# Output tiles of an attention and gated-MLP kernel: separate loads for the last query chunk, late tiles in spare weight buffers, another rule table

## The chip, the core and the metric

The kernel runs on one core of a Trainium2 chip. The metric is the device time of one execution in microseconds (us), lower is better. A profile of one execution shows each engine: PE (TensorE, matmuls), ACT (ScalarE), DVE (VectorE), POOL (GpSimd), SP (SyncE, which issues most DMA transfers).

## What is computed

```python
# x: (1, 2048, 640) bf16;  32 heads of 20;  F = 1728
xn  = layernorm(x)
q, k, v = split_heads(xn @ wqkv)
s   = (softmax(q @ k.T * 20**-0.5) @ v).merge_heads() @ wo
h   = sigmoid(xn @ w_gate) * (xn @ w_up)
g   = silu(h @ w_down)
out = x + s * g
```

The exponentials are the bulk: 32 heads x 2048 queries x 2048 keys. With tiles of 128 keys by 512 queries that is 32 x 4 x 16 = 2048 tiles.

## The kernel before

The kernel works in **blocks**: a block is a group of four heads (`g`, 0 to 7) with a chunk of 512 queries (`c`, 0 to 3), 32 blocks in all. Blocks 0 to 23 go group by group. From block 24 (`PAIR`) on, groups 6 and 7 alternate, so block 25 finishes chunk 0, block 27 chunk 1, block 29 chunk 2 and block 31 chunk 3.

The order of the instructions on PE, ScalarE and VectorE is made when the program is built, by a list scheduler that keeps a clock `now` of its own and rough durations. It chooses for PE among score matmuls ("F"), products with V ("PV") and **filler** items ("M": projections, the MLP, the output projection), and gives each score tile to ScalarE (an exponential, 2 tiles at a time, with a third in a spare PSUM bank when there is one) or to VectorE (`iv`, then three bit-level passes over four tiles). A table `PLAN` holds one row of rules for each block:

```python
RULE = dict(urgent=0.25, rounds=4, hold=0.15, slack=0.2, s0=0.2, s1=0.2, wait3=0.4, fall=1, lag=0.0,
            dmax=2, third=2, dord=0, mord=0, mfew=2, npv=4, held=48, burst=1, excl=1, dl=20, dle=8)
```

For instance, `s0` and `s1` say how far VectorE's queue may reach ahead when it is given a tile, `wait3` how long a fill may wait for a third bank, `mfew` how many PSUM banks filler may take, `lag` how far the filler may be behind.

The output: attention results go to DRAM (`oD`) when a block is normalised, and come back as `o_mid` (chunks 0 to 2) or `o_end` (chunk 3, the first 480 of 640 rows; the rest is done in the tail). The gate values `g` go to DRAM (`gq_dram`) and come back with x in an *out tile*.

```python
    def load_out(tt):                        # out tile of 128 queries: x and the gate
        if tt in out_tiles:
            return
        o2 = xfl[:, tt % 2 * KD * QC:tt % 2 * KD * QC + 3 * D]      # two buffers, in xnT
        ...                                  # two loads on nc.sync
        ev_at[("ol", tt)] = now + 4.0

    def mk_out(tt, h, at):                   # one half of an output tile, chunks 0 to 2
        def alloc():
            if h == 0:
                load_out(tt)
            st["ps"] = misc_ps()
        def mm(kd): ...                      # 5 matmuls 128x320
        def ev():
            ...                              # VectorE: otmp = 0.25 * psum * gate
            ...                              # GpSimd: x + otmp
            if h == 1:
                nc.sync.dma_start(out=out2[...], in_=xr)
                if tt + 2 < TT - 4 and ...:
                    load_out(tt + 2)

    def mk_part(t4, h, at):                  # chunk 3: the first 480 rows of its projection, 4 matmuls
        ...
            nc.vector.scalar_tensor_tensor(out=tmp, in0=st["ps"][:, 0:HD], scalar=0.25, in1=gqr, ...)
            nc.gpsimd.tensor_tensor(out=xps[t4][:, sl], in0=tmp, in1=tail[t4][:, sl], op=ALU.add)
        ...
            pre=[all of chunk 3's down-projection, ("wo",), ("oc", NQC - 1), ("xr",)]
    ...
        if b == NBLK - 2:                    # the parts enter the list of items
```

`xps` lies in the buffer of the down-projection weights, `wd`, once these are no longer needed.

Normalisation of a block (`norm_a`, `norm_b`, `norm_c`): VectorE copies the sums `on` out of PSUM, the denominators go through DRAM, VectorE takes the reciprocal `rt`, this goes through DRAM again and comes back as `rl`; a 1x1 memset on `rl` by VectorE releases GpSimd's multiply `on_bf`, which is stored to `oD`. The times of the steps are set by the scheduler:

```python
    timed.append((free["DVE"] + 7.0, ...) + norm_a(...))            # reciprocal 7 us after the copy
    gos.append((now + GO_AT, tm[1], tm[2], rl))                     # GO_AT = 9.0
    if ... gos[0][0] <= now and (two tiles wait for DVE or now > gos[0][0] + GO_WAIT):   # GO_WAIT = 8.0
```

The tail, after the last exponential: ScalarE copies the last block's sums, PE transposes, VectorE divides, PE transposes back, ScalarE copies (`o7`). Then "early" matmuls (block 30's heads) and "late" ones (block 31's) fill four banks; VectorE and GpSimd combine these with gates, parts and x, and the last tiles are stored. The early matmuls wait until no filler item is left in their bank.

Of the kernel before, what the change touches and what calls it, by code (L numbers as in the profile page):

```python
# [18 lines left out]
P = 128  # L19
HEADS = 32  # L20
GH = 4
NG = HEADS // GH
DH = 20
GC = GH * DH
QC = 512
# [20 lines left out]
    (0.25, 5, 0.15, 0.2, 0.5, 0.2, 0.4, 1, 0.0, 2, 2, 0, 0, 3, 4, 48, 0, 1, 20, 8),  # L46
    (0.25, 5, 0.15, 0.2, 0.5, 0.2, 0.2, 1, 0.0, 2, 2, 0, 0, 3, 4, 48, 0, 0, 20, 8),
    (0.25, 5, 0.15, 0.2, 0.5, 0.2, 0.4, 1, 0.0, 2, 2, 0, 0, 3, 4, 48, 0, 1, 28, 8),
    (0.25, 5, 0.15, 0.2, 0.5, 0.2, 0.4, 1, 14.0, 2, 2, 0, 0, 3, 4, 48, 0, 1, 20, 8),
    (0.25, 5, 0.15, 0.2, 0.5, 0.5, 0.4, 1, 14.0, 2, 2, 0, 0, 3, 4, 48, 0, 1, 20, 8),  # L50
    (0.25, 7, 0.15, 0.2, 0.2, 1.2, 0.4, 1, 0.0, 2, 2, 1, 0, 2, 4, 48, 1, 1, 20, 8),
    (0.25, 5, 0, 0, 0.5, 0.2, 0.4, 1, 14.0, 2, 2, 0, 0, 3, 4, 64, 0, 1, 20, 8),
    (0.25, 5, 0.15, 0.2, 0.5, 0.5, 0.4, 1, 14.0, 2, 2, 0, 0, 3, 4, 48, 0, 1, 28, 8),
    (0.2, 5, 0.15, 0.2, 0.5, 0.5, 0.4, 1, 14.0, 1, 0, 0, 2, 3, 4, 48, 0, 1, 28, 8),
    (0.25, 5, 0.15, 0, 0.5, 0.5, 0.4, 1, 14.0, 2, 2, 0, 0, 3, 4, 48, 0, 1, 28, 8),
    (0.25, 5, 0.15, 0, 0.5, 0.5, 0.4, 1, 14.0, 2, 2, 0, 0, 3, 4, 48, 0, 1, 28, 8),
    (0.25, 5, 0.15, 0, 0.5, 1.2, 0.4, 1, 14.0, 2, 2, 0, 0, 3, 4, 48, 0, 1, 20, 8),
    (0.25, 5, 0.15, 0, 0.5, 1.2, 0.4, 1, 2.0, 2, 2, 0, 1, 3, 4, 48, 0, 1, 20, 8),
    (0.3, 5, 0.15, 0, 0.5, 0.5, 0.4, 1, 14.0, 2, 2, 0, 0, 3, 4, 48, 0, 1, 28, 8),
    (0.25, 5, 0.15, 0, 0.5, 1.2, 0.4, 1, 2.0, 2, 2, 0, 1, 3, 4, 48, 0, 1, 28, 8),  # L60
    (0.3, 5, 0.15, 0.2, 0.5, 0.5, 0.4, 1, 14.0, 2, 2, 0, 0, 3, 4, 48, 0, 1, 28, 8),
    (0.25, 5, 0.15, 0, 0.5, 1.2, 0.4, 1, 4.0, 2, 2, 0, 1, 3, 4, 40, 0, 0, 28, 8),
    (0.25, 5, 0.15, 0, 0.5, 1.2, 0.4, 1, 4.0, 1, 2, 0, 1, 3, 4, 40, 0, 0, 14, 8),
    (0.25, 7, 0.15, 0, 0.5, 1.2, 0.4, 1, 4.0, 1, 2, 0, 1, 3, 4, 40, 0, 0, 14, 8),
    (0.25, 5, 0.15, 0, 0.5, 1.2, 0.4, 1, 4.0, 2, 2, 0, 1, 1, 4, 40, 0, 0, 28, 8),
    (0.2, 5, 0.15, 0, 0.8, 1.2, 0.4, 1, 4.0, 2, 2, 0, 1, 1, 4, 40, 0, 0, 28, 8),
    (0.25, 5, 0.15, 0.5, 0.5, 1.2, 0.4, 1, 4.0, 2, 2, 0, 1, 1, 4, 40, 0, 0, 28, 8),
    (0.25, 5, 0, 0, 0.5, 1.2, 0.4, 1, 4.0, 2, 2, 0, 2, 1, 4, 40, 0, 0, 28, 8),
    (0.25, 5, 0.15, 0, 0.5, 1.2, 0.4, 1, 4.0, 2, 2, 1, 3, 1, 4, 40, 0, 0, 28, 8),
    (0.25, 5, 0.15, 0, 0.5, 1.2, 0.4, 1, 0.0, 2, 0, 1, 3, 1, 4, 40, 0, 0, 28, 8),  # L70
    (0.25, 5, 0.15, 0, 0.2, 1.2, 0.4, 1, 0.0, 2, 0, 1, 3, 1, 4, 40, 1, 0, 28, 8),
    (0.25, 5, 0.15, 0, 0.2, 1.2, 0.4, 1, 0.0, 2, 0, 1, 3, 1, 4, 56, 1, 0, 28, 8),
    (0.25, 5, 0.15, 0, 0, 1.2, 0.4, 1, 0.0, 2, 2, 1, 3, 1, 4, 4, 1, 0, 28, 8),
# [38 lines left out]
def kernel(  # L112
# [11 lines left out]
    nc = tc.nc  # L124
# [360 lines left out]

    def blk(g, c):
        return g * NQC + c if g < NG - 2 else PAIR + 2 * c + g - (NG - 2)
# [297 lines left out]
    def load_out(tt):  # L785
        if tt in out_tiles:
            return
        o2 = xfl[:, tt % 2 * KD * QC:tt % 2 * KD * QC + 3 * D]
        out_tiles[tt] = (o2[:, 0:D], o2[:, D:3 * D].bitcast(FP32))
        nc.sync.dma_start(out=out_tiles[tt][0], in_=x2[tt * P:(tt + 1) * P, :])  # L790
        nc.sync.dma_start(out=out_tiles[tt][1], in_=gq_dram[tt * P:(tt + 1) * P, :])
        ev_at[("ol", tt)] = now + 4.0
# [5 lines left out]
    def mk_out(tt, h, at):  # L798
        st = {}

        def alloc():
            if h == 0:
                load_out(tt)
            st["ps"] = misc_ps()
# [6 lines left out]
        def ev():  # L811
            xr, gqr = out_tiles[tt]
            sl = slice(h * HD, (h + 1) * HD)
            tmp = w2.tile([P, HD], FP32, tag="gqs", bufs=3, name="otmp")
            nc.vector.scalar_tensor_tensor(out=tmp, in0=st["ps"][:, 0:HD], scalar=0.25,  # L815
                                           in1=gqr[:, sl], op0=ALU.mult, op1=ALU.mult)
            add = nc.vector if h == 1 and claimed[0] == NJOB * NBLK else nc.gpsimd
            add.tensor_tensor(out=xr[:, sl], in0=tmp, in1=xr[:, sl], op=ALU.add)  # L818
            if h == 1:
                nc.sync.dma_start(out=out2[tt * P:(tt + 1) * P, :], in_=xr)  # L820
                if tt + 2 < TT - 4 and all(("d", (tt + 2) // 4, t4, i) in ev_at for t4 in range(4) for i in range(2)):
                    load_out(tt + 2)
        return Item([("PE", alloc, [(0.136, lambda kd=kd: mm(kd)) for kd in range(KD)]),
                     ("DVE", 0.40, ev, "free", lambda t: (mark("o", tt, h)(t), pool_hold(t)))], at, need=blk(NG - 1, tt // 4),
                    pre=[("d", tt // 4, t4, i) for t4 in range(4) for i in range(2)] + [("wo",), ("oc", tt // 4)] + (
                        [("o", tt - 2, 1)] if h == 0 and tt > 1 else []), gates={1: [("ol", tt)]})
# [37 lines left out]
    for b in range(NBLK):  # L864
# [20 lines left out]
        if b == NBLK - 2:  # L885
            for t4 in range(4):
                for h in range(2):
                    mk.append(lambda at, t4=t4, h=h: [mk_part(t4, h, at)])
# [231 lines left out]
    with tc.manual_schedule(engines={ENG.PE, ENG.Activation, ENG.DVE}):  # L1120
# [22 lines left out]
        o_next = 0  # L1143
# [41 lines left out]
        while chain or items or glu_items or o_next < NQC or any(it.i < len(it.ops) for it in active):  # L1185
# [10 lines left out]
            if ("wo",) not in ev_at and base() >= PAIR and ("bD", NU - 1) in ev_at and all(  # L1196
# [3 lines left out]
                load_out(0)  # L1200
                load_out(1)
# [5 lines left out]
            if o_next < NQC and o_at.get(blk(NG - 1 if o_next < NQC - 1 else NG - 3, o_next), 1e9) <= now and (  # L1207
                    all(ev_at.get(("o", 4 * o_next - 4 + i, 1), 1e9) <= now for i in range(4)) if 0 < o_next < NQC - 1 else
                    o_next == 0 or all(ev_at.get(("h", 3, kf), 1e9) <= now for kf in range(NFT))):
                o_rows = D if o_next < NQC - 1 else FE  # L1210
                for kd in range(-(-o_rows // P)):
                    r = min(P, o_rows - kd * P)
                    nc.sync.dma_start(out=(o_mid if o_next < NQC - 1 else o_end)[0:r, kd, :],
                                      in_=oD[kd * P:kd * P + r, o_next * QC:(o_next + 1) * QC])
                ev_at[("oc", o_next)] = now + 4.0
                o_next += 1
            if not tail and base() >= NBLK - 4:
                tail_load()
                ev_at[("xr",)] = now + 5.0
            active = [it for it in active if it.i < len(it.ops)]  # L1220
# [19 lines left out]
            for eng in ("ACT", "DVE"):  # L1240
# [8 lines left out]
                if eng == "DVE" and norm_pending is not None and norm_pending[1] <= now and norm_pending[0] < NBLK - 1:  # L1249
                    free["DVE"] = now + T_ON  # L1250
                    timed.append((free["DVE"] + 7.0, norm_pending[0]) + norm_a(norm_pending[0]))
# [4 lines left out]
                if eng == "DVE" and gos and gos[0][0] <= now and (  # L1256
                        sum(x[3] <= now + 0.3 for x in dq) >= 2 or now > gos[0][0] + GO_WAIT):
# [39 lines left out]
                if tm is not None:  # L1297
# [7 lines left out]
                    else:  # L1305
                        gos.append((now + GO_AT, tm[1], tm[2], rl))
# [217 lines left out]
```

## Time and profile before

| | before |
|---|---|
| time, median of 3 | 808.75 us (806.73 to 809.88) |
| profiled span | 804.8 us |
| PE / VectorE / ScalarE / GpSimd busy | 761.6 / 777.5 / 777.7 / 90.5 us |
| mean granted TensorE clock | 0.987 |
| DMA | 62.62 MB, mean 78 GB/s |

In the page, a group's row reads: line, engine, operation, output <- input, shape, count, then busy time in total, mean ns of one, and the engine's idle time before it with what ended it. A window's row gives, for each engine, busy us and the number of instructions, then the granted clock as a share of full speed, the busy share of the DMA engines and GB/s. A timeline's row gives start, duration, engine, line, operation and count; in brackets stands the idle time before it and what ended it.

### The profile page before, as it was taken

To read this page: it belongs to the slowest core of one execution; us is meant where nothing else is said; L and a number is where in the kernel's file an instruction comes from. 1 tells how busy PE (TensorE), PEld (TensorE's weight loads), DVE (VectorE), ACT (ScalarE), POOL (GpSimd) and SP (SyncE) were. 2 spreads that over 40 slices of the span, in tenths; PEclk is the share of its full clock that TensorE was granted. 3 is DMA by queue.
4 is the path that set the end of the run, shared out by engine and by line. 5 is a ranking of instruction groups with operands and counts; after the bars stand their busy time and mean duration, and the time that the engine had idled before them with its cause. 6 is when DMAs were issued, how large, how long until landed. Compare 5 with 4: busy or idle time off the path is not lost.

```text
span 804.8 us, 17176 instructions
## 1 busy us (share of the span) xinstructions
PE 761.6 (95%) x6458; PEld 274.8 (34%) x6514; DVE 777.5 (97%) x1280; ACT 777.7 (97%) x1005; POOL 90.5 (11%) x106
## 2 busy tenths in 40 slices
PE   7899999999999999999999999999999999989795
PEld 6522323233332333344322333343333333322233
DVE  8899999999999999999999999999999999999996
ACT  8899999999999999999999999999999999999892
POOL 6000000000000000000000000000000000411426
PEclk9999999999999999999999999999999999998898
DMA  6511231223122333212223333232143220340522
GB/s 167 172 49 48 68 79 43 70 66 83 56 77 65 79 88 100 69 36 59 62 54 99 84 81 88 60 103 85 46 115 94 48 55 17 89 116 23 176 72 72
DMA packets 95876, 62.62 MB, mean 78 GB/s; under 512 B 36388, under 2 KB 89684, under 8 KB 95792
## 3 DMA queue, kind: packets, MB, share of 16 engines
q1 hardware_dynamic: 95504, 61.18, 27.8%
q8 instruction: 51, 0.84, 0.5%
q14 instruction: 33, 0.27, 0.1%
q10 hardware_dynamic: 288, 0.33, 0.1%
HBM read 47.84 MB, written 13.55 MB: 76 GB/s over the span
## 4 chain that ended last, share of the span: by engine, by line
ACT 66%; PE 22%; issue 5%; DVE 5%; DMA 2%; POOL 0%; SPq 0%; DVEq 0%; ACTq 0%; POOLq 0%
ACT pt L142 59%; PE scA L934 7%; PE bk L970 5%; PE bk L749 5%; ACT tnh L142 3%; PE bk L711 2%; DVE iv L1313 1%; ACT td L142 1%; PE bk L808 1%; DVE pb L1028 1%; ACT sq L338 1%; ACT xnT L362 1%; ACT sq L336 1%; DVE pb L1025 0%; PE bk L934 0%
## 5 line engine op out<-in xcount | busy, mean ns | idle before, releaser
L142 ACT ACTIVATE pt<-scA 128x1024 bf16<-128x1024 f32 x686 | 708.0, 1219 | 6.1 <-PE scA L934 3.1
L1313 DVE TENSOR_SCALAR iv<-bk 128x512 int16<-128x512 f32 x497 | 327.6, 681 | 6.5 <-PE bk L934 4.8
L934 PE MATMUL scA<-q,kT 32*128 32x512 bf16 x1372 | 269.8, 386 | 19.8 <-ACT pt L142 16.1
L934 PE MATMUL bk<-q,kT 32*128 32x512 bf16 x676 | 208.0, 386 | 2.2 <-DVE iv L1313 1.2
L934 PEld LDWEIGHTS <-kT 32*128 32x128 bf16 x2048 | 85.3, 91 | 266.4 <-issue 255.0
L970 PE MATMUL bk<-pt,v 128*21 128x512 bf16 x1551 | 174.8, 385 | 0.1
L1028 DVE TENSOR_TENSOR pb<-iv,pb 128x2048 bf16<-128x2048 bf16 (+1 forms) x125 | 151.6, 1213 | 0.5
L970 PE MATMUL bk<-pb,v 128*21 128x512 bf16 x994 | 149.3, 385 | 0.1
L142 ACT ACTIVATE pt<-bk 128x512 bf16<-128x512 f32 x179 | 142.4, 795 | 0.0
L711 PE MATMUL bk<-xnT,wgu 128*128 128x512 bf16 x486 | 139.1, 382 | 3.2 <-issue 1.9
L1007 POOL TENSOR_TENSOR on_bf<-on,rl 128x512 bf16<-128x512 f32 x31 | 40.3, 1300 | 644.5 <-DVE rl L1005 583.7
L1022 DVE TENSOR_SCALAR pb<-iv 128x2048 int16<-128x2048 int16 (+1 forms) x125 | 86.9, 695 | 0.2
L1025 DVE TENSOR_SCALAR pb<-iv 128x2048 int16<-128x2048 int16 (+1 forms) x125 | 87.0, 696 | 0.0
L749 PE MATMUL bk<-wd,hT 128*128 128x320 bf16 x448 | 84.3, 302 | 0.1
L970 PEld LDWEIGHTS <-v 128*21 128x21 bf16 x2545 | 48.0, 91 | 85.7 <-issue 64.7
L711 PEld LDWEIGHTS <-wgu 128*128 128x128 bf16 x520 | 38.4, 97 | 63.2 <-issue 41.2
L749 PEld LDWEIGHTS <-hT 128*128 128x128 bf16 x448 | 35.2, 97 | 39.9 <-issue 30.5
L142 ACT ACTIVATE tnh<-bk 128x512 bf16<-128x512 f32 (+1 forms) x56 | 45.7, 816 | 0.0
L571 PE MATMUL bk<-xnT,wu 128*128 128x512 bf16 x149 | 43.2, 383 | 1.3 <-issue 1.0
L719 DVE SCALAR_TENSOR_TENSOR hT<-tnh,bk 128x512 bf16<-128x512 bf16 x52 | 35.5, 682 | 1.5 <-PE bk L711 0.5
L818 POOL TENSOR_TENSOR xnT<-otmp,xnT 128x320 bf16<-128x320 f32 x23 | 24.3, 1074 | 57.4 <-DVE otmp L815 52.9
L679 PE MATMUL bk<-wv,xnT 128*128 128x160 bf16 x280 | 26.7, 234 | 0.5 <-DVE iv L1313 0.2
(117 smaller groups left out, 392.8 us busy)
## 6 DMA issues: line engine op xcount, KB each, us to landing
rl<-rd SPq DMA_DIRECT2D x124, 64.0 KB
wgu<-in_B_w_gate_dram SPq DMA_DIRECT2D x24, 320.0 KB
wgu<-in_B_w_up_dram SPq DMA_DIRECT2D x24, 320.0 KB
gq_dram<-gqs SPq DMA_DIRECT2D x24, 160.0 KB
xnT<-gq_dram SPq DMA_DIRECT2D x12, 320.0 KB
xt<-in_A_x_dram SPq DMA_DIRECT2D x16, 160.0 KB
oD<-on_bf SPq DMA_DIRECT2D x120, 20.0 KB
wd<-in_B_w_down_dram SPq DMA_DIRECT2D x1, 2080.0 KB
```

Of the source, the lines that this page charges most:

```text
L142: return nc.scalar.add_instruction(mybir.InstActivation(func=func, name=nc.get_next_instruction_name(), engine=ENG.Activation, ins=[nc.sca ...
L571: nc.tensor.matmul(st["ps"], lhsT=wus[u][:, kd, i, :], rhs=xnT[:, c, kd, :], start=(kd == 0), stop=(kd == KD - 1))
L711: nc.tensor.matmul(st[key][0:fs, :], lhsT=w[:, i, kd, ko * P:ko * P + fs], rhs=xnT[:, c, kd, :], start=(kd == 0), stop=(kd == KD - 1))
L719: nc.vector.scalar_tensor_tensor(out=hT[0:fs, kf, :], in0=st["t"][0:fs, :], scalar=1.0, in1=st["u"][0:fs, :], op0=ALU.add, op1=ALU.mult)
L749: nc.tensor.matmul(st["ps"][:, 0:HD], lhsT=hT[0:fsz[kf], kf, t4 * P:(t4 + 1) * P], rhs=wd[0:fsz[kf], kf, h * HD:(h + 1) * HD], start=(kf = ...
L934: nc.tensor.matmul(dst, lhsT=kTs[gc(b)[0] % 2][32 * j:32 * j + 32, kt * P:(kt + 1) * P], rhs=qts[b % 3][32 * j:32 * j + 32, :], start=True ...
L970: nc.tensor.matmul(bank[pv_bank[0]][32 * j:32 * j + DH + 1, :], lhsT=lhsT, rhs=u["src"], start=first, stop=last, tile_position=(0, 32 * j) ...
L1007: nc.gpsimd.tensor_tensor(out=on_bf, in0=on, in1=rl, op=ALU.mult)
L1022: nc.vector.tensor_scalar(out=pb[:, 0, :, :].bitcast(I16), in0=iv, scalar1=0x7F80, scalar2=1, op0=ALU.bitwise_and, op1=ALU.bitwise_or)
L1025: nc.vector.tensor_scalar(out=pb[:, 1, :, :].bitcast(I16), in0=iv, scalar1=0x007F, scalar2=0x3F00, op0=ALU.bitwise_and, op1=ALU.bitwise_or)
L1028: nc.vector.tensor_tensor(out=pb[:, 1, :, :], in0=iv.bitcast(BF16), in1=pb[:, 1, :, :], op=ALU.mult)
L1313: nc.vector.tensor_scalar(out=d["iv"][:, j, :], in0=bank[bk], scalar1=B_OFF, scalar2=0.0, op0=ALU.add, op1=ALU.max)
```

## The change

It takes apart things that were tied to one another near the end. Chunk 3's `o_end` is loaded as soon as the groups concerned are done, and no longer after chunk 2's `o_mid`. Out tiles are loaded by a counter of their own (`l_next`) when a buffer comes free, and no longer from within an item. Tiles 10 and 11 get buffers in the spare part of `wd`. The parts enter the list three blocks sooner. The normalisation of blocks 25, 27, 29 and 31 ("pressing") is given shorter times. And 28 of the 32 rows of `PLAN` (rows 4 to 31) are replaced by rows chosen with the TensorE's activity-dependent clock in mind.

```diff
 PLAN = (
     (rows 0 to 3 unchanged)
-    (0.25, 5, 0.15, 0.2, 0.5, 0.2, 0.4, 1, 0.0, 2, 2, 0, 0, 3, 4, 48, 0, 1, 20, 8),
+    (0.25, 5, 0.3, 0.2, 0.8, 0.2, 0.4, 1, 0.0, 2, 2, 0, 0, 3, 4, 40, 0, 1, 20, 8),
     ... (26 more rows) ...
-    (0.25, 5, 0.15, 0, 0, 1.2, 0.4, 1, 0.0, 2, 2, 1, 3, 1, 4, 4, 1, 0, 28, 8),
+    (0.25, 4, 0.15, 0, 0.2, 0.5, 0, 1, 8.0, 2, 1, 2, 2, 1, 4, 32, 1, 1, 20, 16),
 )
+    def pressing(b):
+        return b >= PAIR and b % 2 == 1
     def load_out(tt):
-        if tt in out_tiles:
-            return
         o2 = xfl[:, tt % 2 * KD * QC:tt % 2 * KD * QC + 3 * D]
+        if tt >= TT - 6:
+            o2 = wd.rearrange("p k e -> p (k e)")[:, 8 * D + (tt - TT + 6) * 3 * D:8 * D + (tt - TT + 7) * 3 * D]
     ... mk_out:
-            if h == 0:
-                load_out(tt)
-                if tt + 2 < TT - 4 and all(("d", (tt + 2) // 4, t4, i) in ev_at for t4 in range(4) for i in range(2)):
-                    load_out(tt + 2)
-                    pre=[("d", tt // 4, t4, i) for t4 in range(4) for i in range(2)] + [("wo",), ("oc", tt // 4)] + (
-                        [("o", tt - 2, 1)] if h == 0 and tt > 1 else []), gates={1: [("ol", tt)]})
+                    pre=[("oc", tt // 4), ("ol", tt)])
-        if b == NBLK - 2:
+        if b == NBLK - 5:
             (the parts enter the list)
     ... main loop:
-                load_out(0)
-                load_out(1)
     (the loads of o_mid, now for chunks 0 to 2 alone)
-            if not tail and base() >= NBLK - 4:
+            if ("oc", NQC - 1) not in ev_at and ("wo",) in ev_at and o_at.get(blk(NG - 3, NQC - 1), 1e9) <= now and all(
+                    ev_at.get(("h", NQC - 1, kf), 1e9) <= now for kf in range(NFT)):
                 tail_load()
                 ev_at[("xr",)] = now + 5.0
+                (the loads of o_end)
+                ev_at[("oc", NQC - 1)] = now + 6.0
+            if l_next < TT - 4 and ("wo",) in ev_at and (
+                    l_next < 2 or l_next >= TT - 6 or ev_at.get(("o", l_next - 2, 1), 1e9) <= now) and all(
+                    ev_at.get(("d", NQC - 1 if l_next >= TT - 6 else l_next // 4, t4, i), 1e9) <= now
+                    for t4 in range(4) for i in range(2)):
+                load_out(l_next)
+                l_next += 1
-                    timed.append((free["DVE"] + 7.0, norm_pending[0]) + norm_a(norm_pending[0]))
+                    timed.append((free["DVE"] + (5.5 if pressing(norm_pending[0]) else 7.0), norm_pending[0]) + norm_a(norm_pending[0]))
-                        ... or now > gos[0][0] + GO_WAIT):
+                        ... or now > gos[0][0] + (1.5 if pressing(gos[0][1]) else GO_WAIT)):
-                        gos.append((now + GO_AT, tm[1], tm[2], rl))
+                        gos.append((now + (7.0 if pressing(tm[1]) else GO_AT), tm[1], tm[2], rl))
```

## The prediction, made before the changed kernel was run

> **What bounds the kernel now.** I read the page's totals first, then the windows by stage, then the waits and the timeline of the stretches that the windows marked. The totals:
>
> ```profile
> span 804.8 us, 17176 instructions
> PE 761.6 (95%) x6458; PEld 274.8 (34%) x6514; DVE 777.5 (97%) x1280; ACT 777.7 (97%) x1005; POOL 90.5 (11%) x106
> L142 ACT ACTIVATE pt<-scA 128x1024 bf16<-128x1024 f32 x686 | 708.0, 1219 | 6.1 <-PE scA L934 3.1
> L1313 DVE TENSOR_SCALAR iv<-bk 128x512 int16<-128x512 f32 x497 | 327.6, 681 | 6.5 <-PE bk L934 4.8
> L142 ACT ACTIVATE pt<-bk 128x512 bf16<-128x512 f32 x179 | 142.4, 795 | 0.0
> ```
>
> Three engines are nearly full, and the exponentials fill two of them. ScalarE does 686x2 + 179 = 1551 score tiles (128 keys by 512 queries), VectorE the other 497: together 2048, all there are. ScalarE and VectorE are each idle for about 27 us of 804.8, so that is the whole budget of a change which only moves work. It lies as follows, from the windows by stage (which the reader can sum): ScalarE 7.3 us and VectorE 6.1 us before 40 us (start-up), practically nothing of ScalarE from 40 to 650 us (0.2 us in 400 to 500, else full), and the rest at the end. The end, in stretches of 4 us; the columns are busy us of PE, of the weight load, of VectorE, ScalarE and GpSimd, then the granted TensorE clock:
>
> ```profile
> 716.00:720.00 4.00, 3.77 (x42) 1.10 (x41) 3.85 (x8) 4.00 (x6) 0.51 (x1) 1.00 0.08 22
> 720.00:724.00 4.00, 2.00 (x9) 0.40 (x9) 3.95 (x7) 4.00 (x6) 0.76 (x1) 0.74 0.11 27
> 724.00:728.00 4.00, 2.64 (x14) 0.58 (x14) 4.00 (x8) 4.00 (x6) 0.00 (x0) 0.50 0.12 35
> 728.00:732.00 4.00, 3.69 (x20) 0.86 (x17) 3.02 (x5) 3.25 (x4) 0.00 (x0) 0.50 0.23 60
> ...
> 752.00:756.00 4.00, 2.00 (x12) 0.58 (x12) 3.13 (x4) 4.00 (x5) 2.91 (x4) 1.00 0.47 154
> 756.00:760.00 4.00, 2.25 (x14) 0.42 (x11) 4.00 (x5) 2.82 (x4) 1.21 (x2) 0.51 0.87 269
> 760.00:764.00 4.00, 4.00 (x37) 0.73 (x37) 3.55 (x8) 2.97 (x4) 1.27 (x1) 0.64 0.40 119
> ```
>
> The reader is to see a sequence. At 720 PE runs out of filler and is half idle, though ScalarE and VectorE stay full. After that the clock is 0.50, and only when PE gets work again, at half speed, do ScalarE and VectorE run dry (728 to 732: 0.75 and 0.98 us). The same recurs at 752 to 764. The timeline says what filler was missing. No down-projection or output matmul stands between 717.5 and 729.4, nor between 751.2 and 772.2. These lines end the droughts:
>
> ```profile
> 719.33 0.06 DVE L1005 MEMSET rl<- 1x1 f32 x1
> 720.79 1.40 SPq L1015 DMA_DIRECT2D oD<-on_bf  x4
> 723.39 0.35 SPq L1213 DMA_DIRECT2D v<-oD  x1
> 729.37 1.25 PE L808 MATMUL bk<-xnT,v 128*128 128x320 bf16 x4
> ```
>
> The output projection of chunk 1 can start only after block 27 is normalised. Its copy from PSUM is at 699.28, the multiply it waits for is released at 719.33, 20 us later, and the way through DRAM takes 10 us more. Meanwhile all of the "part" matmuls (480 rows of the last chunk's projection) are held back by the schedule until 787.9, where PE is 100% busy (780 to 792). There they delay the tail:
>
> ```profile
> 788.71 1.13 PE L841 MATMUL bk<-xnT 128*128 128x320 bf16 x7
> 789.77 0.39 PE L970 MATMUL bk<-pb,v 128*21 128x512 bf16 x1
> 790.24 0.59 ACT L1067 COPY on<-bk 128x512 f32<-128x512 f32 x1 [1.91 <-issue]
> 792.93 0.58 ACT L1084 COPY o<-scA 80x512 bf16<-80x512 bf16 x1 [2.11 <-PE scA L1080]
> 796.02 0.76 DVE L1104 SCALAR_TENSOR_TENSOR hT<-bk,gql 128x256 f32<-128x256 f32 x2 [1.12 <-PE bk L1062]
> ```
>
> ScalarE's copy ends at 793.51, but VectorE starts the last combination only at 796.02: in between PE finishes the parts (to 794.1) and then the early matmuls that had to wait for their banks.
>
> **What the Trainium skill says.** "TensorE: Matmul & The Clock Gate", section "What's actually happening", says that about 3.4 us without enough PE activity put the clock to half, and about 3.4 us of activity bring it back. The trace agrees in kind: 2.00 of 4 us busy from 720 on, then 0.50 until past 732. "Perfetto Trace Analysis", "Identifying the Most-Contended Engine", warns that matmul busy time overstates how full PE is; here the half clock shows it, since PE is 4.00 of 4 us busy at 760 to 764 while its users starve. "DMA: Bandwidth & Descriptors", "Anatomy of one DMA", gives about 2 us fixed per transfer, mostly completion; here the chain of waits has 3.05 us for an out tile's gate load and 2.99 us for its x load, so a load that starts when its item does is not hidden. "GPSIMD Engine Reference", "1. Specifications", says that GpSimd shares SBUF interfaces with VectorE. The trace fits: the two 128x2048 mask passes take 852 and 793 ns in 720 to 760, where GpSimd adds out tiles, against 684 and 679 ns in 500 to 600.
>
> **The change, part by part.** The arithmetic stays what it was: as many score tiles, output matmuls, adds and transfers. Only places and times move.
>
> 1. *Parts earlier.* Their items enter the list at block 27 instead of 30, and the load of their input no longer queues behind chunk 2's. They still need chunk 3's down-projection, which ended at 717.7. They are 32 matmuls, busy 0.45 + 1.13 + 0.99 + 1.26 + 1.40 = 5.2 us on PE by the timeline. From 720 to 728 PE is idle for 2.00 + 1.36 = 3.4 us, and just there they become ready. At the end, PE gets 5.2 us back. If the early matmuls are done when ScalarE's copy ends (793.51), the late ones can run at once and VectorE starts near 794.1 instead of 796.02: 1.9 us. The last PV matmul at 789.77 also no longer stands behind a run of parts that began at 788.71: its operand was written by 788.98, so about 0.5 us. Everything after is a fixed chain. Sum **2.4 us**; I take 2.0, since something else (the last out tiles) can stand there.
>
> 2. *Normalisation of the odd late blocks sooner.* From copy to multiply it took 22.6 us (650.22 to 672.79), 20.1 (699.28 to 719.33) and 19.2 (742.67 to 761.9). The new constants ask for 0.7 + 5.5 + 0.25 + 7.0 and at most 1.5 more, so at most 15 us. Chunk 1's output work becomes ready about 5 us sooner (near 724 instead of 729) and chunk 2's about 4 us (near 768 instead of 772).
>
> 3. *Out tiles loaded ahead, the last two in spare weight space.* It removes VectorE's 1.25 us wait on a gate load at 698 and GpSimd's waits on x loads (3.45 and 1.07 us near 752 to 755). GpSimd is 11% busy, so of its waits only what holds a buffer counts: the "otmp" waits of VectorE on GpSimd, 1.3 us. On the end this is small, some **0.3 us**, but it lets parts 1 and 2 take effect.
>
> 4. *28 of 32 rows of the rule table.* Without building it, its order can't be seen. What it can win is what the idle times are worth. From the timeline, 28 pairs on ScalarE in 25.84 us are 0.461 us per tile, 2.17 tiles per us. From the page, VectorE's tile is (327.6 + 151.6 + 86.9 + 87.0)/497 = 1.314 us, 0.76 tiles per us. Together 2.93, so a us of idle ScalarE costs 0.74 us at the end and one of VectorE 0.26 us. From 720 to 770, ScalarE is idle 1.00 + 1.18 + 1.03 = 3.21 us and VectorE 1.59 + 1.13 + 0.45 = 3.17 us (windows): 3.21 x 0.74 + 3.17 x 0.26 = **3.2 us**. That is all the clock drop costs, much less than the time at half clock, 8 x (0.26 + 0.50 + 0.50 + 0.49 + 0.36) = 17 us by the clock column, suggests. I take two thirds, 2.1 us, because the filler left after 717 (some 17 us of PE time) can't cover every hole in 70 us. Elsewhere, from 100 to 650, ScalarE is full. VectorE's idle share of 1 to 2.3% (0.8 to 2.3 us per 100 us) sums to 8.8 us, worth 2.3 us if all went. The new rows no longer hold a fill for a third bank (wait3 0 from row 9 on), so there are fewer single-tile exponentials; a triple costs 1.40 us (785.15 to 786.55), 0.467 per tile, hardly more than a pair. I book 0 to 0.5 us gain here and an uncertainty of 2 us both ways.
>
> Sum: 2.0 + 2.1 + 0.3 + 0.3 = 4.7 us, so 808.75 - 4.7 = **804.0 us**.
>
> **Rivals.** *A new drought elsewhere.* If the parts fill 718 to 728 and chunk 1's outputs follow directly, the next stretch has less filler than now (chunk 1's outputs filled 729 to 751), and the clock could drop around 740 to 764 for longer. For it: total filler is unchanged. Against: the rows were chosen with the clock in mind, and one drop costs only about 1.6 us. The time would be 807 to 809. *The rows make the main stretch worse.* 600 us run under new rows; if VectorE took 10 tiles fewer, ScalarE would need 4.6 us more, less the VectorE time freed: up to 812. Against: VectorE is already 98% busy there, and I assume that the rows were tuned for this very order. *The rows make it better.* With the 2.3 us of VectorE idle recovered and the droughts gone entirely, 808.75 - 2.4 - 3.2 - 2.3 - 0.3 = 800.5. *Loads were hidden anyway.* Then parts 1 and 3 bring only the tail, and the time is near 806.
>
> **Range and chances.** The centre is 804.0; the optimistic rival gives 800.5 and the pessimistic one 812. Launch-to-launch spread of the kernel before is 806.73 to 809.88, so I widen a little: 798.5 to 810.5 for 8 in 10. Faster by over 2% means below 792.6, over 16 us, more than all the idle time after 650 us; 0.03. Slower by over 2% means above 824.9, possible only if PE stays at half clock for long; 0.02. Within 2%: 0.95.
>
> **What would show it.** Part 1: the part matmuls run near 715 to 735, none after 785, and VectorE's first combination follows ScalarE's last copy by under 1 us. Part 2: 15 us or less from copy to multiply in blocks 25, 27, 29. Part 4: the clock of 720 to 764 stays at 1.00 and ScalarE's idle from 650 to 788 falls from 4.35 us to under 2. The prediction is wrong if VectorE's count of tiles falls well below 497 with the main stretch longer, or if the span from the last exponential to the end (788.3 to 804.8, 16.5 us) doesn't shrink.

## The result, and the profile after

| | before | after |
|---|---|---|
| time, median (range; launches) | 807.77 us (806.73 to 809.88; 4) | 800.76 us (799.92 to 802.10; 4) |
| ratio | | 0.9911 [0.9884, 0.9939] |
| profiled span | 804.8 us | 799.5 us |
| ScalarE's last exponential ends | 788.33 us | 785.06 us |
| from there to the end (the tail) | 16.47 us | 14.44 us |
| idle 650 us to last exponential: ScalarE, VectorE | 4.36, 5.58 us | 0.68, 1.65 us |
| TensorE at half clock in that stretch | 17.0 us | none |

The changed kernel is 0.9% faster. The totals and the three rows of score tiles on its page, against those shown of before:

```profile
span 799.5 us, 17203 instructions
...
PE 765.9 (96%) x6513; PEld 275.3 (34%) x6513; DVE 776.4 (97%) x1278; ACT 777.2 (97%) x1002; POOL 90.9 (11%) x104
...
L142 ACT ACTIVATE pt<-scA 128x1024 bf16<-128x1024 f32 x690 | 710.9, 1231 | 2.5 <-PE bk L932 2.2
L1316 DVE TENSOR_SCALAR iv<-bk 128x512 int16<-128x512 f32 x496 | 325.3, 679 | 5.0 <-PE bk L932 3.5
...
L142 ACT ACTIVATE pt<-bk 128x512 bf16<-128x512 f32 x172 | 137.9, 802 | 0.0
```

The division of the tiles is the same but for one: 690x2 + 172 = 1552 on ScalarE, 496 on VectorE (before 1551 and 497). Busy times hardly move. What has gone is waiting: the exponentials' idle time before them falls from 6.1 to 2.5 us. The windows say where (busy us of PE, weight load, VectorE, ScalarE, GpSimd, then the granted clock):

```profile
720.00:724.00 4.00, 3.73 (x31) 1.58 (x27) 4.00 (x8) 4.00 (x6) 0.22 (x1) 1.00 0.01 2
724.00:728.00 4.00, 3.99 (x31) 1.93 (x28) 3.99 (x8) 4.00 (x7) 2.95 (x3) 1.00 0.38 109
728.00:732.00 4.00, 4.00 (x40) 1.38 (x42) 3.88 (x7) 4.00 (x6) 1.32 (x2) 1.00 0.51 154
...
756.00:760.00 4.00, 3.72 (x33) 1.31 (x29) 3.86 (x8) 4.00 (x7) 0.00 (x0) 1.00 0.15 49
760.00:764.00 4.00, 4.00 (x32) 1.23 (x30) 4.00 (x5) 4.00 (x5) 2.47 (x2) 1.00 0.52 150
```

ScalarE is busy without a break in all five, where before it lost up to 1.18 us in a window, and the clock stays at 1.00. What fills PE there is in the timeline:

```profile
721.89 0.85 PE L809 MATMUL bk<-xnT,v 128*128 128x320 bf16 x5
...
749.73 1.26 PE L752 MATMUL bk<-wd,hT 128*128 128x320 bf16 x8
...
756.11 0.68 PE L752 MATMUL bk<-wd,hT 128*128 128x320 bf16 x3
...
758.55 0.43 PE L839 MATMUL bk<-xnT 128*128 128x320 bf16 x2
```

L752 is the down-projection of chunk 3, whose last matmul ended at 716.6 before the change (the prediction read 717.5) and which is now spread until 756.8. L809, chunk 1's output matmuls, begin at 721.89 instead of 729.37. L839 are the parts, now at 758.55 to 772.2 instead of 787.9 to 794. After 700 us the longest stretch without any of these three is 5.1 us (751.0 to 756.1). Before, there were two of 12.8 and of 21.0 us. The tail, in the timeline:

```profile
786.25 0.59 ACT L1065 COPY on<-bk 128x512 f32<-128x512 f32 x1 [1.18 <-issue]
...
789.31 0.58 ACT L1082 COPY o<-scA 80x512 bf16<-80x512 bf16 x1 [2.47 <-PE scA L1078]
...
791.09 0.76 DVE L1102 SCALAR_TENSOR_TENSOR hT<-bk,gql 128x256 f32<-128x256 f32 x2 [0.59 <-PE bk L1060]
```

From the end of ScalarE's copy (789.89) to the first combination it takes 1.20 us, before 2.51.

### The profile page after: what moved, and what is told of

It reads as the page before. It is cut to its first block, busy times and chain, and to the rows that moved or that the text cites. A ratio compares the mean times of both kernels' runs of the same rounds, so it can differ in the third digit from the quotient of the medians.

```text
span 799.5 us, 17203 instructions
## 1 busy us (share of the span) xinstructions
PE 765.9 (96%) x6513; PEld 275.3 (34%) x6513; DVE 776.4 (97%) x1278; ACT 777.2 (97%) x1002; POOL 90.9 (11%) x104
## 4 chain that ended last, share of the span: by engine, by line
ACT 36%; PE 20%; DVE 10%; issue 2%; DMA 0%; SPq 0%; DVEq 0%; ACTq 0%
ACT pt L142 33%; PE scA L932 6%; PE bk L714 4%; PE bk L968 3%; DVE iv L1316 3%; PE bk L752 3%; DVE pb L1026 2%; ACT tnh L142 2%; DVE pb L1023 1%; PE bk L809 1%; DVE pb L1020 1%; ACT td L142 1%; PE bk L574 1%; PE bk L682 1%; PE bk L839 1%
## 5 line engine op out<-in xcount | busy, mean ns | idle before, releaser
L932 PE MATMUL bk<-q,kT 32*128 32x512 bf16 x668 | 205.1, 383 | 0.2
L968 PE MATMUL bk<-pb,v 128*21 128x512 bf16 x992 | 153.6, 382 | 0.8 <-DVE pb L1026 0.8
L1026 DVE TENSOR_TENSOR pb<-iv,pb 128x2048 bf16<-128x2048 bf16 x124 | 151.7, 1223 | 0.7
L714 PE MATMUL bk<-xnT,wgu 128*128 128x512 bf16 x520 | 145.0, 382 | 1.0 <-DVE iv L1316 0.4
L142 ACT ACTIVATE pt<-bk 128x512 bf16<-128x512 f32 x172 | 137.9, 802 | 0.0
L1020 DVE TENSOR_SCALAR pb<-iv 128x2048 int16<-128x2048 int16 x124 | 87.5, 705 | 0.0
L1023 DVE TENSOR_SCALAR pb<-iv 128x2048 int16<-128x2048 int16 x124 | 86.3, 696 | 0.0
L752 PE MATMUL bk<-wd,hT 128*128 128x320 bf16 x448 | 84.5, 302 | 0.3 <-DVE gql L768 0.2
L752 PEld LDWEIGHTS <-hT 128*128 128x128 bf16 x448 | 35.4, 97 | 40.2 <-issue 30.7
L574 PE MATMUL bk<-xnT,wu 128*128 128x512 bf16 x160 | 45.7, 382 | 0.9 <-DVE qu L622 0.5
L819 POOL TENSOR_TENSOR xnT<-otmp,xnT 128x320 bf16<-128x320 f32 x19 | 20.6, 1089 | 55.1 <-DVE otmp L816 44.4
```

Of the source, the lines that this page charges most:

```text
L142: return nc.scalar.add_instruction(mybir.InstActivation(func=func, name=nc.get_next_instruction_name(), engine=ENG.Activation, ins=[nc.sca ...
L574: nc.tensor.matmul(st["ps"], lhsT=wus[u][:, kd, i, :], rhs=xnT[:, c, kd, :], start=(kd == 0), stop=(kd == KD - 1))
L714: nc.tensor.matmul(st[key][0:fs, :], lhsT=w[:, i, kd, ko * P:ko * P + fs], rhs=xnT[:, c, kd, :], start=(kd == 0), stop=(kd == KD - 1))
L752: nc.tensor.matmul(st["ps"][:, 0:HD], lhsT=hT[0:fsz[kf], kf, t4 * P:(t4 + 1) * P], rhs=wd[0:fsz[kf], kf, h * HD:(h + 1) * HD], start=(kf = ...
L932: nc.tensor.matmul(dst, lhsT=kTs[gc(b)[0] % 2][32 * j:32 * j + 32, kt * P:(kt + 1) * P], rhs=qts[b % 3][32 * j:32 * j + 32, :], start=True ...
L968: nc.tensor.matmul(bank[pv_bank[0]][32 * j:32 * j + DH + 1, :], lhsT=lhsT, rhs=u["src"], start=first, stop=last, tile_position=(0, 32 * j) ...
```

## Experiments

The question was which part of the change earns the gain: the rule table, the structure around it (loads, buffers, parts, normalisation), or only both together; and how the gain divides between clock, idle engines and tail. Ratios are to the kernel before, run on the same chip beside each experiment.

### The table and the structure apart

All 32 rows of the old table in the changed kernel:

```diff
 PLAN = (
-    (rows 4 to 31 of the changed kernel)
+    (rows 4 to 31 of the kernel before)
```

> The changed kernel with the 32 old rows of PLAN: only the structure is new. Theory A (the structure makes the gain: parts, out tiles and normalisation can move, the rows only fit them): about 803, the parts run before 735 and the span from the last exponential to the end falls from 16.5 us to 14.5. Rival B (the rows make it, because they ration the down-projections of chunk 3 so that PE has filler up to 756): 806 to 809, the down-projections end near 717 as before and the TensorE clock falls below 0.8 somewhere between 720 and 770.

Measured: 809.83 us, ratio 1.0033 [1.0017, 1.0049], the rival's case and slightly slower still. The whole gain is gone and a little more. Its windows in the drought and in the tail:

```profile
756.00:760.00 4.00, 2.86 (x19) 0.60 (x20) 3.56 (x7) 4.00 (x5) 1.27 (x1) 0.52 0.77 231
760.00:764.00 4.00, 4.00 (x39) 0.66 (x31) 3.63 (x6) 2.66 (x4) 0.00 (x0) 0.63 0.22 58
...
796.00:800.00 4.00, 4.00 (x19) 2.01 (x17) 0.94 (x3) 0.58 (x1) 0.60 (x1) 0.50 0.00 0
```

The first drought of before, at 720, is absent: the parts stand at 718.5 to 728.8 and chunk 1's outputs follow at once, as the prediction had imagined. But then everything is used up early. The down-projection ends at 715.7, chunk 1's outputs at 753.3, and nothing comes until chunk 2's at 769.57. PE is half idle, the clock drops to 0.52, and when work returns ScalarE is busy for 2.66 of 4 us. At 703.97 VectorE waits 1.51 us for `lt`, which the shorter normalisation asks for sooner, and ScalarE then 0.77 us. The last exponential still ends at 786.57, sooner than before, but the tail grows to 21.03 us. ScalarE waits 6.39 us for the last block's sums, since VectorE's passes for its last tiles run to 792.2, and by then PE has been idle so long that the last matmuls run at 0.50.

The reverse, the new table in the kernel before:

```diff
 PLAN = (
-    (rows 4 to 31 of the kernel before)
+    (rows 4 to 31 of the changed kernel)
```

> The kernel before with the 32 new rows of PLAN, without the new structure: the parts still enter at block 30 and chunk 3's input is loaded after chunk 2's. Theory A: 806 to 809, since the parts stand in the tail again (16 us from the last exponential to the end). Rival B (the rows alone make it): 801 to 803, with the clock at 1.00 from 700 to 780.

Measured: 813.85 us, 1.0070 [1.0044, 1.0096]: the table alone loses, more than either theory said. (The profile is of the slowest of six launches, 815.88.) It does ration the down-projection (to 764.7), and there is no drought at 720 to 764. But then nothing is left until 779.5, because the old structure loads the parts' input only after chunk 2's, and the clock is 0.50 in 768 to 776. The end is worse still; its timeline:

```profile
793.62 0.58 ACT L1084 COPY o<-scA 80x512 bf16<-80x512 bf16 x1 [3.01 <-PE scA L1080]
...
797.39 0.49 DVE L818 TENSOR_TENSOR xnT<-otmp,xnT 128x320 bf16<-128x320 f32 x1 [3.50 <-DMA xnT<-in_A_x_dram]
...
798.33 5.49 PE L841 MATMUL bk<-xnT 128*128 128x320 bf16 x20 [3.54 <-DVE otmp L847]
...
805.76 0.76 DVE L1104 SCALAR_TENSOR_TENSOR hT<-bk,gql 128x256 f32<-128x256 f32 x2 [1.34 <-PE bk L1062]
```

ScalarE is done at 794.2, yet the first combination comes at 805.76. In between the last out tile's x load is waited for (3.50 us on VectorE, which holds up PE's parts for 3.54), and then 20 part matmuls take 5.49 us at half clock. Earlier, at 700.06, VectorE waits 2.14 us for a gate load, and ScalarE loses 2.47 us in three holes from there to 705.2. So what the structure gives seems to be chiefly that parts and out tiles don't hang on late loads.

In these two profiles, table and structure alone both reach the last exponential sooner (786.57 and 787.83) than the kernel before (788.33). What each loses, it loses in the tail: 21.03 and 26.3 us against 16.47.

Rows 0 to 19 old, 20 to 31 new, in the changed kernel:

```diff
 PLAN = (
-    (rows 4 to 19 of the changed kernel)
+    (rows 4 to 19 of the kernel before)
     (rows 20 to 31 of the changed kernel)
```

> The changed kernel with old rows for blocks 0 to 19 and new rows for 20 to 31. If the main stretch gained nothing from its rows, 800 to 802, like the changed kernel. If the 8 score tiles that the changed kernel is ahead at 700 us come from the rows of the main stretch, 803 to 805.

Measured: 809.10 us, 1.0018 [1.0005, 1.0031], slower than both cases expected. It arrives at 650 us with 1675 score tiles begun (after 1681, before 1677) and 2 `tanh` activations more than the changed kernel, so the main stretch is not where it loses much. A first loss follows at once: the clock is 0.65 at 660 to 664, and ScalarE waits 1.34 us for PE. Then the late rows, though unchanged, now meet another state of the lists: outputs end at 755.1, the next come at 770.0, and the clock falls to about 0.75 in that drought and to half in the tail. The rows seem to fit one exact course of the schedule.

Over these kernels one pattern holds: each stretch of more than 11 us after 700 us without down-projection, output or part matmuls brings a drop of the clock (12.8 and 21.0 us before, 16.3 with the old table, 14.8 with the table alone, 14.9 with the mixed rows). The changed kernel has none over 5.1 us and no drop before the tail. Drops without such a stretch exist too: 0.66 at 748 to 752 with the old table, 0.75 at 700 to 704 with the table alone, 0.65 at 660 to 664 with the mixed rows. No run varied such a stretch alone.

### What the clock is worth

The kernel before, with 55 idle matmuls (their results are never read) put in where PE finds nothing to do in the last blocks, and the order of all else unchanged:

```diff
+                elif nxt is None and cur is None and base() >= NBLK - 5 and ... now >= warm_at[0] and ...:
+                    nc.tensor.matmul(bank[f], lhsT=ident, rhs=wo[0][:, 0:512], start=True, stop=True)
+                    warm_at[0] = now + 0.3
```

> The kernel before, same order, with 55 matmuls 128x512 of no use added on PE into free PSUM banks where the scheduler gives PE nothing to do, in the last five blocks. They keep PE active in the droughts and do no work. If the loss of 728 to 732 and 756 to 764 comes from the half clock, the clock stays at 1.00, and the last exponential comes up to 3.2 us sooner: 804.5 to 806.5. If it comes from filler pushed to a time when PE is full, whatever the clock, nothing is gained: 807 to 809.

Measured: 806.31 us, 0.9976 [0.9964, 0.9989], so 1.9 us of 807.69 (0.9 to 2.9). Two of its windows:

```profile
724.00:728.00 4.00, 4.00 (x24) 1.14 (x23) 3.80 (x7) 3.85 (x5) 0.00 (x0) 1.00 0.12 35
...
756.00:760.00 4.00, 3.17 (x16) 0.82 (x16) 4.00 (x5) 2.99 (x4) 1.54 (x2) 1.00 0.81 230
```

The clock is 1.00 throughout 720 to 770, yet ScalarE is still idle for 1.97 us there (before 3.21) and VectorE for 2.71 (3.17). By the prediction's rates the difference is worth 1.24 x 0.74 + 0.46 x 0.26 = 1.0 us, inside the interval.

Which waits went says more. After 650 us ScalarE has four holes in the kernel before: 1.15 us at 700.40, 1.00 in two pieces at 731.3 and 732.5, 1.18 at 759.55, and 0.98 in two pieces at 762.1 and 763.6. With the clock held, the second and the fourth shrink to 0.17 and 0.16 us. The first and the third stay, 1.18 and 1.21 us, so the clock alone does not make them. These lines of the kernel before show where they come from:

```profile
698.27 0.49 DVE L815 SCALAR_TENSOR_TENSOR otmp<-bk,xnT 128x320 f32<-128x320 f32 x1 [1.25 <-DMA xnT<-gq_dram]
698.82 0.37 PE L934 MATMUL bk<-q,kT 32*128 32x512 bf16 x1 [0.94 <-DVE otmp L815]
...
758.41 0.61 PE L934 MATMUL bk<-q,kT 32*128 32x512 bf16 x2 [1.22 <-DVE iv L1313]
```

In the first, VectorE waits for an out tile's gate load, PE's score matmuls wait for the bank that VectorE should free, and ScalarE waits for them. In the third, PE waits for VectorE's `iv`, which comes late after two passes of 1.28 and 1.27 us (684 and 679 ns in 500 to 600) beside GpSimd's out-tile adds. In the kernel with idle matmuls PE waits there too, 0.83 us, and then three idle matmuls (759.07 to 759.89) stand before the next score pair. So the 1.9 us is, if anything, less than what the clock costs. What holding back filler earns beyond a warm PE was not measured apart.

The idle matmuls also steady the kernel: 22 launches lie within 2.3 us (805.38 to 807.72), 57 of the kernel before within 6.5 (805.45 to 811.95). So the clock accounts for about 1 to 3 us of the kernel before, and waits behind VectorE and late loads for up to about as much (worked out under step 3 below).

### The small parts

Each was undone alone in the changed kernel: the shorter normalisation times, the parts' place in the list, the spare buffers for the last two out tiles.

```diff
-        return b >= PAIR and b % 2 == 1
+        return False
```

> The changed kernel with the old times of normalisation for blocks 25, 27 and 29 too (about 20 us from copy to multiply instead of 13 to 16). Theory A (there is other filler, down-projections up to 756 and parts up to 772, so chunk 1 and 2 may come later): 800.5 to 802. Rival B (the output work of chunk 2 is pushed into the tail): 804 to 807, with output matmuls after ScalarE's last copy.

Measured: 802.44 us, 0.9922 [0.9899, 0.9945]. From copy to memset it takes 23.1 and 26.5 us in blocks 27 and 29 (after 15.6 and 13.4). The clock dips once, to 0.75 at 772 to 776, and ScalarE's late idle time is 1.56 us instead of 0.68.

```diff
-        if b == NBLK - 5:
+        if b == NBLK - 2:
             (the parts enter the list)
```

> The changed kernel with the parts entering the list at block 30 as before, not 27. In the changed kernel they ran only from 758 to 772. Theory A (their earlier entry is not used, the down-projections stand before them): 800 to 802. Rival B, step 1 of the prediction (their entry is what frees the tail): parts run after 785 and the time is 803 or more.

Measured: 802.93 us, 0.9925 [0.9896, 0.9954]. The parts run at 758.1 to 771.1, as in the changed kernel, except the last four matmuls, which slip to 789.45; the tail is 15.77 us. So the number of the block matters for four matmuls of 32, and these alone fall into the tail. What lets the others run before chunk 2's outputs is, by the code, that their input no longer queues behind chunk 2's, which this kernel keeps; no run undid that alone.

```diff
-        if tt >= TT - 6:
-            o2 = wd....
-                    l_next < 2 or l_next >= TT - 6 or ev_at.get(("o", l_next - 2, 1), 1e9) <= now) and all(
-                    ev_at.get(("d", NQC - 1 if l_next >= TT - 6 else l_next // 4, t4, i), 1e9) <= now
+                    l_next < 2 or ev_at.get(("o", l_next - 2, 1), 1e9) <= now) and all(
+                    ev_at.get(("d", l_next // 4, t4, i), 1e9) <= now
```

> The changed kernel without the spare weight space: out tiles 10 and 11 use the two old buffers, and are loaded only when tiles 8 and 9 are done. Theory A (they matter, as tile 8 is done only near 781 and 9 near 786): VectorE waits for loads of 2 to 3 us in the tail, 803.5 to 807. Rival B (hidden): 800 to 802.

Measured: 803.08 us, 0.9923 [0.9900, 0.9946]. In the tail the waits on loads are back (VectorE 1.8 us on a gate load and 0.5 on an x load, GpSimd 4.6 on an x load), and the tail is 16.86 us, 2.4 more, but the last exponential ends 0.9 us earlier. All three times lie between the ranges of their two theories, and all three intervals overlap with that of the change. Each part seems to be worth a microsecond or so; none is resolved.

### The last row: how long VectorE takes score tiles

The old table's long tail, with VectorE's leftover passes, suggested that its last number, `dle`, mattered. VectorE gets tiles of the last block only while at least `dle` are left. The old table has 8, the new one 16. The changed kernel with 8:

```diff
-    (0.25, 4, 0.15, 0, 0.2, 0.5, 0, 1, 8.0, 2, 1, 2, 2, 1, 4, 32, 1, 1, 20, 16),
+    (0.25, 4, 0.15, 0, 0.2, 0.5, 0, 1, 8.0, 2, 1, 2, 2, 1, 4, 32, 1, 1, 20, 8),
```

> The changed kernel with one number of the table changed back: in the last block VectorE may take tiles down to 8 left (dle 8) instead of 16. It takes two more tiles. Theory A (VectorE's last tile sets the start of the tail, as in the kernel with the old table, where ScalarE waited 6.4 us): ScalarE's copy comes 1.5 to 3 us later, 802.5 to 804. Rival B (ScalarE is relieved by as much): 800 to 801.5.

Measured: 807.07 us, 0.9973 [0.9956, 0.9991], beyond what either theory allowed. One number takes back some 5 of the 7 us. Up to 760 us the two kernels are alike, and the last exponential ends even 0.7 us sooner (784.35). The tail is 21.55 us instead of 14.44; its timeline:

```profile
790.91 0.69 DVE L1026 TENSOR_TENSOR pb<-iv,pb 128x1024 bf16<-128x1024 bf16 x1
...
792.12 0.59 ACT L1065 COPY on<-bk 128x512 f32<-128x512 f32 x1 [7.76 <-PE bk L968]
...
797.20 1.06 PE L1060 MATMUL scA<-wo_t,o 80*128 80x512 bf16 x2
...
797.45 0.76 DVE L1102 SCALAR_TENSOR_TENSOR hT<-bk,gql 128x256 f32<-128x256 f32 x2 [3.16 <-PE bk L1060]
```

VectorE has 498 tiles, two more than after, and finishes their passes only at 791.6, between the output tiles' adds. ScalarE waits 7.76 us for the sums. PE, half idle meanwhile (2.34 of 4 us busy in 788 to 792), falls to 0.50 in 796 to 800, so a pair of 512-wide matmuls takes 1.06 us instead of 0.59, and the combination waits 3.16 us.

If that explained the old table's loss, 16 in its last row should mend it, in the changed structure or in the kernel before:

```diff
 changed kernel with the old table:
-    (0.25, 5, 0.15, 0, 0, 1.2, 0.4, 1, 0.0, 2, 2, 1, 3, 1, 4, 4, 1, 0, 28, 8),
+    (0.25, 5, 0.15, 0, 0, 1.2, 0.4, 1, 0.0, 2, 2, 1, 3, 1, 4, 4, 1, 0, 28, 16),
```

> The changed kernel with the 32 old rows, but dle 16 in the last one. VectorE then ends the last block on a full group of four tiles; with dle 8 it had a group of two left over, whose three passes start only when all tiles are given out, and ScalarE waited 6.4 us. Theory A (the left-over group of the last block is the main cost of the old table): ScalarE's copy within 2.5 us of its last exponential, 803.5 to 806. Rival B (the drought of 748 to 764 and the other rows set the end): 808 or more.

Measured: 809.28 us, 1.0013 [0.9991, 1.0035]. The tail falls from 21.03 to 17.12 us, as that theory says, but the time doesn't. In this profile the last exponential ends 4 us later (790.58): there is an extra stall at 704 to 716, with a wait of 1.9 us on the load of `lt` and a clock of 0.50, besides the drought at 756 to 764. The order of the work is the same up to the last block, so that stall differs between launches: with dle 8 the same wait for `lt` was 1.51 us and cost ScalarE 0.77. The tail alone isn't what the old table costs, for even the lower end, 0.9991, lies far above the change's 0.9911.

```diff
 kernel before:
-    (0.25, 5, 0.15, 0, 0, 1.2, 0.4, 1, 0.0, 2, 2, 1, 3, 1, 4, 4, 1, 0, 28, 8),
+    (0.25, 5, 0.15, 0, 0, 1.2, 0.4, 1, 0.0, 2, 2, 1, 3, 1, 4, 4, 1, 0, 28, 16),
```

> The kernel before with dle 16 in the last row, nothing else. Its left-over group has one tile and its parts fill PE meanwhile, so ScalarE's copy came only 1.95 us after its last exponential. Theory A (the left-over group costs only what stands out beyond the other work of the tail): 806 to 807.5. Rival B (this number alone makes most of the gain in any kernel): 802 to 804.5. Rival C (nothing): 807.5 to 808.5.

Measured: 809.73 us, 1.0014 [1.0002, 1.0027]. No gain, if anything a loss. The tail hardly changes (16.05 us, before 16.47): near its start VectorE waits 1.95 and 0.55 us for PE's output work, so VectorE is not what holds it.

Is 16 in the changed kernel good because no small group of tiles is left over, or because VectorE gets few tiles so late? With 24, VectorE has 494 tiles, and again a leftover group of two:

```diff
-    (0.25, 4, 0.15, 0, 0.2, 0.5, 0, 1, 8.0, 2, 1, 2, 2, 1, 4, 32, 1, 1, 20, 16),
+    (0.25, 4, 0.15, 0, 0.2, 0.5, 0, 1, 8.0, 2, 1, 2, 2, 1, 4, 32, 1, 1, 20, 24),
```

> The changed kernel with dle 24 instead of 16: VectorE takes two tiles fewer than in the changed kernel (494 instead of 496), but again ends with a left-over group of two. Theory A (it is the left-over group, not the amount, that delays the tail): the copy comes 3 us or more after the last exponential, 804 to 807.5. Rival B (VectorE's amount of work in the last block): as fast as the changed kernel or faster, 799.5 to 801.5.

Measured: 801.97 us, 0.9921 [0.9899, 0.9943], its interval overlapping the change's. The group's last pass and the copy:

```profile
786.16 0.69 DVE L1026 TENSOR_TENSOR pb<-iv,pb 128x1024 bf16<-128x1024 bf16 x1
...
787.82 0.59 ACT L1065 COPY on<-bk 128x512 f32<-128x512 f32 x1 [2.29 <-PE bk L968]
```

The same pass of the same size stands at 786.16 instead of 790.91, and ScalarE waits 2.29 us instead of 7.76. So a leftover group alone costs about a microsecond of waiting (1.18 us in the changed kernel, 2.29 here). The larger cost with 8 is that VectorE has more tiles so late than it can finish beside the output work. From 494 to 498 tiles are 4 x 1.31 = 5.3 us of its time (an estimate with the prediction's time for a tile), and with 24 it is even idle for 1.97 us before 781.19. Whether the amount or the lateness counts was not separated.

Last, the old table with 16 and idle matmuls as above (42 of them, at least 0.15 us apart instead of 0.3), to see what remains when the clock is held:

```diff
+                    nc.tensor.matmul(bank[f], lhsT=ident, rhs=wo[0][:, 0:512], start=True, stop=True)
+                    warm_at[0] = now + 0.15
```

> The changed kernel with the old rows, dle 16 in the last one, and 42 matmuls 128x512 of no use on PE where the scheduler gives it nothing to do in the last five blocks (none of them in the tail). Theory A (what the old rows cost in the new structure is the clock drop near 756 to 770 and VectorE's late last tiles, both repaired here): the clock stays near 1.00 up to the last exponential, which ends at 785.5 to 787; with a tail of about 17 us 802.5 to 805.5, and the launches lie within 3 us of one another, where the kernel without these matmuls had 8.7 us. Rival B (the order that the other new rows give can't be had otherwise): 807 or more.

Measured: 808.52 us, 1.0000 [0.9984, 1.0015], and the launches lie within 5.6 us, not within 3. This doesn't answer the question. The clock is 1.00 from 748 to 764, but the dose was too large; the timeline shows it:

```profile
757.18 0.39 PE L932 MATMUL scA<-q,kT 32*128 32x512 bf16 x2
...
757.51 1.25 PE L1488 MATMUL bk<-xnT,ident 128*128 128x512 bf16 x5
...
758.69 0.39 PE L932 MATMUL scA<-q,kT 32*128 32x512 bf16 x2
```

Five idle matmuls (L1488) take 1.25 us between two score steps and stretch the step to 1.51 us, longer than the exponential of a pair needs (1.02). ScalarE then waits for them, at full clock. Earlier, after a wait of 1.70 us for `lt` at 704.00, it loses 2.28 us up to 710.6, with the clock at 0.75 in 708 to 712. All three kernels with the old table in the changed structure have this wait, and the changed kernel has not. Whether the shorter normalisation times cause it could be seen from the old table in the structure without them; that was not run.

## Why the prediction was right, step by step

The time, 800.76, lies in the range of 798.5 to 810.5, 3.2 us under the centre. The profiles account for 5.3 us against 4.7 predicted: 3.27 up to the last exponential and 2.03 in the tail. The other 1.7 us of the 7.0 between the medians is in the choice of launches: the profiled one of before took 806.51 us, 1.26 under its median, that of after 801.21, 0.45 over.

1. **Parts earlier, 2.0 us: the size right, the place wrong.** The tail shrank by 2.03 us: 1.31 between ScalarE's copy and the first combination (2.51 to 1.20), where 1.9 was booked, 0.35 before (5.18 to 4.83) and 0.37 after (8.78 to 8.41), which had been called fixed. Under 1 us from the copy to the combination didn't come, for the reason given: the last out tiles stand there now (VectorE's adds to 790.5). The parts didn't fill 720 to 728; they run at 758.55 to 772.2. Only the old table puts them at 718.5, and that kernel is the one with the long drought later. None after 785 was right.

2. **Normalisation at most 15 us: nearly.** From the copy to the memset that releases the multiply 15.6, 15.6 and 13.4 us. Chunk 1's outputs start at 721.9 (predicted 724), chunk 2's at 772.0 and not 768, since the parts stand before them. The step's worth isn't resolved.

3. **Out tiles ahead, 0.3 us: far too small.** The prediction saw VectorE's 1.25 us wait for a gate load at 698, but not that ScalarE then stands still for 1.15 us. It also saw GpSimd's 3.45 us wait for an x load and VectorE's wait of 1.10 us for GpSimd at 752.84, but booked the 1.18 us of ScalarE at 759.55, which follow, to the clock. At its own rates these are worth (1.15 + 1.18) x 0.74 + (1.25 + 1.10) x 0.26 = 2.3 us, or somewhat less, as the clock has a part in the second hole. All four profiled kernels with the old loading have the first hole (VectorE waits 1.07 to 2.14 us, ScalarE then 0.96 to 2.47). The changed kernel has neither. That the earlier loads remove them is read from the traces. The run with two buffers gave back the loads of the last two tiles alone (its profile is 1.5 us longer; the intervals overlap).

4. **The rule table, 2.1 of 3.2 us: the size nearly right, the reasons not.** The exchange rates roughly held: 3.68 us less idle time on ScalarE and 3.93 on VectorE are worth 3.68 x 0.74 + 3.93 x 0.26 = 3.7 us, and the last exponential came 3.27 us sooner. But "all the clock drop costs" was not 3.2 us, since most of the hole at 759.55 isn't the clock's. The two holes that shrink with the clock held have 1.98 us of ScalarE and, with VectorE's idle time beside them (1.99 us), are worth at most 2.0 us. And they went wholly, not by two thirds. The reason given, that the filler left after 717 can't cover every hole, took that amount as given. The new table moves filler: 43 down-projection matmuls, 8.3 us of PE, run after 720, before the change none. In exchange a hole of 0.68 us is new at 766.0 (0.5 us), where PE waits 0.85 us for VectorE's `iv`, after a pass of 1.76 us beside GpSimd's multiply.

5. **Main stretch, 0.3 us: none.** At 650 us the change has begun 4 tiles more, but 4 of the 56 `tanh` activations fewer. Its idle time up to there is longer: ScalarE 8.33 us (before 7.46), VectorE 17.13 (15.55), of which 0.72 and 0.80 us more lie before 40 us, where the rows are the same. That 3.27 falls short of 3.7 fits a small loss there, well within the 2 us allowed.

So the sum came out near partly by luck: up to 2 us missing in step 3 are offset in part by the new hole of 0.5 us and by a main stretch that gave nothing.

The optimistic rival's 800.5 us was almost hit, but not on its grounds: it needed 2.3 us of VectorE's idle time between 100 and 650, and that idle time rose, from 8.8 to 9.6 us. The rival of a new drought elsewhere (807 to 809) didn't come true for the change, but the old table in the new structure (809.83) is just that case: parts at 718, outputs directly after, clock down at 748 to 764. The rules and the structure need each other. Alone, either loses; together they gain 0.9%. Which rows do it stays open: only whole tables, one mix and the last number were tried.

## What to carry to other kernels

When an engine stands still while the clock is low, don't put it all down to the clock: hold the clock up once, and see which waits stay. Here half of ScalarE's stayed, behind VectorE and late loads. Where PE's filler work comes in bursts, spread it: hold back what is ready early so that no stretch lacks it, and see to it that the next filler doesn't queue behind an unrelated load. A tuned table and the structure it was tuned on are one object, to be changed and judged together; a row carried over can lose what it won elsewhere. In the last block, stop giving work to the engine with the long chain early enough, for a few tiles too many there can cost more than they save (here 5 us against 0.7). In another schedule the same number changed nothing.

## What the runs showed of the hardware that was not expected

- PE at half clock for 17 us cost only about 1 to 3 us here. ScalarE stays full from 720 to 728, at clocks of 0.74 and 0.50, and loses time only from 728 on, when PE has more to do again.
- How long the half clock lasts differs from launch to launch. The kernel before with `dle` 16 gives ScalarE the same work in the same order up to 781.9. In its profile the clock is 0.50 until 736 (before: 0.98 in 732 to 736), and ScalarE loses 2.38 us there instead of 1.00 and 1.87 instead of 0.98 after 762. That may be much of the spread of 6.5 us, which idle matmuls cut to 2.3. But the old table with idle matmuls still spreads over 5.6 us.
- The clock bites in the tail too. The Trainium skill ("TensorE: Matmul & The Clock Gate", "What's actually happening") gives about 3.4 us of idling as enough to halve it. With `dle` at 8, PE is 2.34 and 2.35 of 4 us busy from 788 to 796, and 0.50 follows from 796. So about half busy was not enough to keep it warm, as at 720 in the kernel before (2.00 and 2.64 of 4 us).
- GpSimd and VectorE can slow each other a good deal. The Trainium skill ("GPSIMD Engine Reference", "1. Specifications") says that they share SBUF interfaces, and that it is VectorE instructions in a two-port mode or with two SBUF inputs that contend; it gives no size there. In the changed kernel the 128x2048 pass with two inputs takes 2.17 us at 783.31, when GpSimd's 128x512 multiply has been running since 782.69, and 1.21 at 779.66, where it begins before GpSimd's add. That add, begun at 779.82, takes 1.70 us; one at 765.43 takes 0.79. At 761.33 the multiply begins first and takes 1.27 us, and the pass begun at 761.39 takes 1.76 (0.67 at 777.93). So in these three pairs the one that begins second is the slow one. No run was made on it.
